# Linear attention with a Mish block on one core: denominators of the first block in front of kv, modulation's columns later, norms moved between engines

## The chip, the cores and the metric

The kernel runs on one core of one Trainium2 chip. The core has TensorE (matrix products), VectorE, ScalarE and GpSimd (work on tiles of 128 partitions), and SyncE, whose queue only starts transfers. The profile calls them PE, DVE, ACT, POOL and SP; PEld is TensorE's loading of the stationary operand. Each engine takes its instructions in the order in which the program issues them, and waits on semaphores for what other engines and transfers deliver. The metric is the device time of one execution in microseconds (us), lower is better.

## The reference

S = 2048 rows, D = 512 columns, F = 1792, 32 heads of 16. Cut to what matters:

```python
mod = (silu(c) @ w_mod).reshape(1, 6, 1, -1)
sa, ca, ga, sb, cb, gb = (mod[:, i] for i in range(6))
h = layernorm(x) * (1 + ca) + sa
q, k, v = heads(h @ wqkv)
pq, pk = phi(q), phi(k)                  # phi(t) = where(t > 0, t + 1, exp(t)) + 1e-6
kv = einsum("bhsd,bhse->bhde", pk, v)
z = einsum("bhsd->bhd", pk)
o = einsum("bhqd,bhde->bhqe", pq, kv) / (einsum("bhqd,bhd->bhq", pq, z)[..., None] + 1e-6)
x = x + ga * (merge(o) @ wo)
h = layernorm(x) * (1 + cb) + sb
x = x + gb * (mish(h @ w1 + b1) @ w2)
```

## The kernel before

The 2048 rows are four blocks b = 0 to 3 of 512, each of four tiles t of 128 rows by 512 columns. Nearly every tile in SBUF comes from one pool of 101 buffers of 2 KB a partition (`sb`), so a load can wait until an older tile is no longer read. PSUM has eight banks in three groups: "acc" (4), "h" (3) and "tp" (1). Products are made in three passes from a high and a low half of each operand: `mm3` multiplies high by high, high by low and low by high. `split` makes the halves: ScalarE copies the high half, and one step later VectorE subtracts it from the operand to get the low half (names ending in h and l).

The order of work is written out by hand. Work beside the products is written as generators; `spawn` puts one in a list, and `tick()`, which stands between the units of TensorE's work, runs each listed generator on to its next `yield`, in the order of spawning. `spawn_idle` does the same for work that comes at the end of each tick. So the position of a `yield`, of a `spawn` or of a call decides where an instruction stands in its engine's queue.

The stages:

1. The block 0 norm, its K, and then for b = 1 to 3 the K products (`k_unit`), phi of K, and the sum of K's outer products with the normalized x (`g_unit`, in four "acc" banks, gacc). `ln_side(b)` (L423) normalizes block b's x beside the products of the block before: statistics on VectorE, the power -1/2 on GpSimd (`ln_rstd`, L199), the apply on ScalarE (`ln_apply`, L208; its other form, L210, is VectorE's). The transposes of block b + 1 (`transpose`, L237) read all four tiles.
2. `q_sevens` makes Q of blocks 0 and 1 together, in seven products instead of eight per pair of halves. A partial product stays in its bank; VectorE reads it (cq, L356), and then another product is added onto the same bank. `beside_q(n)` is called between those products: it starts loads of x, spawns `kv_side` and `mod_side`, and ticks. `mod_side(order, per)` loads columns of `w_mod` and, three ticks after a load, reduces each on VectorE to a column of mc (`mod_col`, L175, out wm). After column 23 it spawns `bcast_row`, which transposes gb on TensorE (bank "tp"), copies it on ScalarE and sends it out and back through two GpSimd transfers, to have gb on all partitions; after column 19 it makes 1 + cb.
3. The masked product kv (kv_ps, L940, then two VectorE passes, L943) and its split. Then Q of block 2 (`q_unit(2, g)`), beside it the denominators of blocks 0 and 1, and m = kv times wo (m_ps). `attend(b, wait, queue)` (L784) is a generator: first 32 small products on TensorE sum q over the heads (den, L789, bank "tp"); then VectorE adds a constant and takes the reciprocal (L793, L794), one transfer writes it to DRAM (rden_d, L796), and four transfers read it back, spread over 16 partitions a head (rd, L800), both on `queue`, GpSimd's if none is named; after `wait` more ticks VectorE multiplies q by rd (L808) and the result is split (qs).
4. Q of block 3, in its middle the output units of block 0 (`o_unit`, out o: 12 matmuls of qs by m); `norm_first` and `norm_each` norm the result for the Mish block, with sums by ScalarE (`act_sums`, L220, L221) and GpSimd's power. `rows(g, wait)` (L686) loads two column groups of w1 on SyncE's queue, waits that many steps, makes their sums on VectorE (L697 to L700) and splits them; `early_rows` holds the first two.
5. The output units of blocks 1 to 3, and then the Mish block. `pair_unit(0, g, ...)` makes two column groups of blocks 0 and 1 in seven products, again adding products onto banks that VectorE has read (cb, L1044); `two_pairs` interleaves the first two pairs. Beside each pair run `w2_job` (w2 times gb, stored to DRAM), `rows` of a later pair, the second products (`d_unit`, oacc), and `norm_tile` for one of the eight tiles of blocks 2 and 3: tiles with even t on ScalarE (sums, then the apply), with odd t on VectorE (statistics, then the apply). `norm_next()` spawns the next one: at the start of each pair from the third on (g = 2 and up), and in `trail`, whose unit runs late in a pair. After the last pair the normed tiles are read back.
6. The same products for blocks 2 and 3, and the second product of those in sevenths.

Of the kernel before, what the change touches and what calls it, by code (L numbers as in the profile page):

```python
# [25 lines left out]
def block_kernel(ctx: ExitStack, tc: tile.TileContext, x, wqkv, wo, w1, b1t, w2, c, wmodt, out):  # L26
    nc = tc.nc
    act, dve, pool, pe, sp = nc.scalar, nc.vector, nc.gpsimd, nc.tensor, nc.sync
# [13 lines left out]
    def ps(tag, name, shape=(P, 512)):  # L42
        return psp.tile(list(shape), F32, tag=tag, name=name, bufs=PBUFS[tag])
# [6 lines left out]
    def spawn(gen):  # L50
        fresh.append(iter(gen))

    def spawn_idle(gen):

        idle_work.append(gen)
# [45 lines left out]
    def load_wmod(i):  # L101
        wm[i] = sb(f"wm_{i}")
        sp.dma_start(wm[i], wmodt[P * i:P * (i + 1), :])
# [102 lines left out]
    def ln_apply(key, b, j, t, dst, engine):  # L206
        if engine is act:
            act.activation(dst, t, AF.Identity, bias=nb[key, b][:, j:j + 1], scale=rs[key, b][:, j:j + 1])  # L208
        else:
            engine.tensor_scalar(dst, t, mv[key, b][:, j, 0:1], rs[key, b][:, j:j + 1],  # L210
                                 op0=ALU.subtract, op1=ALU.mult)
# [195 lines left out]
    def mod_side(order, per):  # L407

        steps = [order[n:n + per] for n in range(0, len(order), per)]
        for n in range(len(steps) + 3):  # L410
            for i in steps[n] if n < len(steps) else ():
                load_wmod(i)
            if n >= 3:
                for i in steps[n - 3]:
                    mod_col(i, sc_row)
                    for lo, name in (8, "ga"), (20, "gb"):
                        if i == lo + 3:
                            spawn(bcast_row(lo, name))
                    if i == 19:
                        plus_one(16, 20)  # L420
            yield

    def ln_side(b):  # L423
        for j in range(4):
            ln_stats("x", b, j, xt["x", b, j])
            if j == 3:
                ln_eps("x", b)
                ln_rstd("x", b)
            yield
        ln_shift("x", b)  # L430
        for j in range(4):
            t = xt["x", b, j]
            ln_apply("x", b, j, t, t, act)
            if j % 2:
                yield

# [249 lines left out]
    def rows(g, wait):  # L686

        r = [sb(f"w1p_{g}_{i}", F32, (P, 4, P)) for i in range(2)]
        for i in range(2):
            f = 2 * g + i  # L690
            sp.dma_start(r[i], w1[:, P * f:P * (f + 1)].rearrange("(k p) f -> p k f", p=P))
        for _ in range(wait):
            yield
        a11, a12, a21, a22 = [r[i][:, 2 * k:2 * k + 2, :] for i in range(2) for k in range(2)]
        s12, s34 = [sb(f"s{n}_{g}", F32, (P, 4, P)) for n in (12, 34)]
        s1, s2, s3, s4 = s12[:, 0:2, :], s12[:, 2:4, :], s34[:, 0:2, :], s34[:, 2:4, :]
        dve.tensor_tensor(s1, a21, a22, op=ALU.add)  # L697
        dve.tensor_tensor(s2, s1, a11, op=ALU.subtract)
        dve.tensor_tensor(s3, a11, a21, op=ALU.subtract)
        dve.tensor_tensor(s4, a12, s2, op=ALU.subtract)  # L700
        yield
        keep, todo = {}, []
        op_rows[g] = keep
        for name, v, parts in (("a1", r[0], ("a11", "a12")), ("s12", s12, ("s1", "s2")), ("s34", s34, ("s3", "s4")),
                               ("a22", a22, ("a22",))):
            half = split(f"{name}_{g}", v, keep, name)
            next(half)
            todo.append((name, half, parts))
            if len(todo) == 2:
                yield  # L710
                for name, half, parts in todo:
                    run(half)
                    for i, part in enumerate(parts):
                        op_a[g, part] = [h[:, 2 * i:2 * i + 2, :] for h in keep[name]]
                todo = []
# [16 lines left out]
            for i, part in enumerate(parts):  # L732
                op_a[g, part] = [h[:, 2 * i:2 * i + 2, :] for h in halves]

    early_rows = [rows(g, 1) for g in range(2)]

    for b in range(1, NB):
        last = b == NB - 1
# [45 lines left out]
    def attend(b, wait, queue=pool):  # L784

        p = ps("tp", f"den_{b}")[:, 0:P]
        for g in range(4):
            for t in range(4):
                pe.matmul(p[32 * t:32 * (t + 1), :], hmask[:, g, :], pq[b, g][:, P * t:P * (t + 1)],  # L789
                          start=g == 0, stop=g == 3)  # L790
        yield
        rden = cst.tile([P, P], F32, tag="rden", name=f"rden_{b}", bufs=2)
        dve.tensor_scalar(rden, p, tiny_den[:, 0:1], 1.0, op0=ALU.add, op1=ALU.mult)  # L793
        dve.reciprocal(rden, rden)  # L794
        d = drp.tile([32, 512], F32, name=f"rden_d_{b}")
        queue.dma_start(bass.AP(tensor=d.tensor, offset=d.offset, ap=[[P, 4], [512, 32], [1, P]]), rden)  # L796
        rd = []
        for g in range(4):
            r = sb(f"rd_{b}_{g}")
            queue.dma_start(r, bass.AP(tensor=d.tensor, offset=d.offset + 8 * g * 512,  # L800
                                     ap=[[512, 8], [0, 16], [1, 512]]))
            rd.append(r)
        for _ in range(wait):
            yield
        parts = []
        for g in range(4):
            t = pq[b, g]
            dve.scalar_tensor_tensor(t, t, TINY, rd[g], op0=ALU.add, op1=ALU.mult)  # L808
            parts.append(split(f"qs_{b}_{g}", t, qs, (b, g)))
            next(parts[-1])  # L810
            if g % 2:
                yield
                run(parts.pop(0))
                run(parts.pop(0))
# [100 lines left out]
    def kv_side():  # L915

        for k in range(4):
            dve.scalar_tensor_tensor(zs[k], gacc[k], mc[:, 4 + k:5 + k], zs[k], op0=ALU.mult, op1=ALU.add)
            if k % 2:
                yield  # L920

    def beside_q(n):
        if n < 4:
            load_x(1, n, "r")
        else:
            load_x(2, n - 4, "r")
        if n == 1:
            spawn(kv_side())
            spawn(mod_side([20, 21, 22, 23, 16, 17, 18, 19], 2))
        tick()  # L930

    q_sevens(beside_q)
    load_x(2, 3, "r")
    kvs = {}
    kv_ps = ps("acc", "kv_ps")
    for g in range(4):
        for k in range(4):
# [6 lines left out]
                          kv_ps.rearrange("p (g m) -> p g m", g=4)[js, :, js],  # L944
                          bmask[js, js].unsqueeze(1).to_broadcast([64, 4, 64]), op=ALU.mult)
    spawn(split("kv", kv, kvs, 0))
    attending = attend(0, 3)
    for g in range(4):
        q_unit(2, g)
        if g == 0:  # L950
            next(attending)
            next(attending)
        if g == 1:
            spawn(attending)
        if g == 2:
            spawn(attend(1, 4))
        if g == 1:
            spawn(mod_side(range(12, 16), 1))
        load_x(3, g, "r")
        if g == 2:  # L960
            for k in range(4):
                m_ps = ps("acc", f"m_ps_{k}")
                mm3(m_ps, [h[:, P * k:P * (k + 1)] for h in kvs[0]], wos[k], True, True)
                spawn(split(f"m_{k}", m_ps, ms, k))
        tick()
    for g in range(4):
        q_unit(3, g)
        tick()
        if g == 1:
            for t in range(4):  # L970
                o_unit(0, t)
                spawn(norm_first(t))
                if t == 1:
                    spawn(attend(2, 5))
                tick()
            spawn_idle(early_rows[1])
    act.preload_act_table_set("mish")

    order = {8: [(0, 0), (0, 2)], 9: [(0, 1)], 10: [(0, 3), (1, 0)], 11: [(1, 2)], 12: [(1, 1)], 13: [(1, 3)]}
    for b in range(1, NB):  # L980
        for t in range(4):
            n = 4 * b + t
# [180 lines left out]
    begun = [pair_begin(0, g, ("tp" if g else "h", "acc")) for g in range(2)]  # L1163
# [8 lines left out]
    def norm_next():  # L1172
        if tiles:
            spawn(tiles.pop(0))

    def trail(f, side=None):
        def unit():
            if side is not None:
                norm_next()
                spawn(side)  # L1180
            d_unit(0, f, f)
            ahead(1, f)
        return unit

    for g in range(1, G):
        for f in (2 * g, 2 * g + 1):
            spawn(w2_job(f))
        if g == 1:
            two_pairs(0, 0, 1, begun, (lambda: None, trail(0, rows(3, 2))))
            store_rows(0)  # L1190
        else:
            norm_next()
            pair_unit(0, g, g % 2, (trail(2 * g - 3), trail(2 * g - 2, rows(g + 2, 2) if g + 2 < G else ())))
        if g < KEPT:
            store_rows(g)
        if g == G - 1:
            for n in range(8):
                load_back("n", nd, 2 + n // 4, n % 4)
# [104 lines left out]
    for n, g in enumerate(pairs):  # L1303
# [18 lines left out]
        if n == 0:  # L1322
            begun = [pair_begin(L, pairs[i], ("tp" if i else "h", "acc")) for i in range(2)]
# [79 lines left out]
```

## Time and profile before

| | before |
|---|---|
| median of 3 runs (lowest to highest) | 502.89 us (502.24 to 505.9) |
| the profiled execution | 501.73 us, span 499.9 us |
| granted TensorE clock in it | 1.00 |
| DMA packets, bytes, mean rate | 66765, 98.58 MB, 197 GB/s |

The profiled execution's own time is its span and the 1.8 us around it. Lines of the timeline read: start, duration, engine, line, operation, out<-in, shape, count, and in brackets the idle time of that engine before the instruction and what ended it. Times count from the span's start. A matmul's end is modelled, so start times are what can be compared.

The page's row of TensorE's busy time in 40 equal slices, and of the DMA engines':

```profile
PE   7999999999998999999999999999999999999997
...
DMA  8714544157556407279799887989997614688512
```

Each digit is the busy share of 12.5 us in tenths. TensorE is at 9 nearly throughout; the transfers are light from 25 to 180 us, where the attention is computed, and heavy from 230 to 375 us, in the Mish block.

### The profile page before, as it was taken

The page shows a single profiled execution, that of the slowest core. Times are in us where ns is not written, and L with a number is a line of the kernel's source. Part 1 is how long each engine was busy: PE and PEld are TensorE (multiplying, and loading weights), DVE is VectorE, ACT ScalarE, POOL GpSimd, SP SyncE. Part 2 cuts the span into 40 slices and gives each one's busy share as a digit, 9 for nine tenths or more (in the row PEclk, how much of TensorE's full clock was granted, in tenths as well). Part 3 has the DMA queues.
Part 4 walks back from the last instruction along what each step waited for, and adds up shares of the span by engine and source line. Part 5 has one row for each costly group of instructions (what it writes and reads, how often), then busy time and mean ns, then how long its engine had stood idle before and what let it go on. Part 6 is the DMA issues. An engine that isn't in the chain of part 4 may idle for free.

```text
span 499.9 us, 7705 instructions
## 1 busy us (share of the span) xinstructions
PE 489.5 (98%) x2640; PEld 411.1 (82%) x2640; DVE 367.9 (74%) x713; ACT 298.7 (60%) x535; POOL 145.2 (29%) x246
## 2 busy tenths in 40 slices
PE   7999999999998999999999999999999999999997
PEld 6787888877786878887888888888788888899997
DVE  6886888999759599977777663679832666759871
ACT  6878587866453879747776655278154555568200
POOL 4573120000022414103224415124554400445200
PEclk9999999999999999999999999999999999999999
DMA  8714544157556407279799887989997614688512
GB/s 310 280 43 113 140 118 93 49 146 249 171 132 156 118 18 251 88 259 358 259 346 333 292 258 195 356 239 372 388 339 190 190 45 126 164 216 224 135 43 85
DMA packets 66765, 98.58 MB, mean 197 GB/s; under 512 B 7405, under 2 KB 31861, under 8 KB 66726
## 3 DMA queue, kind: packets, MB, share of 16 engines
q0 software_dynamic: 29360, 45.31, 33.3%
q1 hardware_dynamic: 37220, 52.51, 31.7%
q8 instruction: 21, 0.34, 0.3%
q10 hardware_dynamic: 146, 0.26, 0.1%
q14 instruction: 18, 0.15, 0.1%
HBM read 62.92 MB, written 33.03 MB: 192 GB/s over the span
## 4 chain that ended last, share of the span: by engine, by line
PE 80%; DVE 10%; ACT 4%; DMA 3%; issue 1%; POOL 1%; POOLq 0%; DVEq 0%; ACTq 0%
PE p_a L1039 18%; PE p_s L1039 7%; PE oacc L76 5%; PE oacc L75 5%; PE oacc L74 5%; PE m L76 5%; PE m L75 5%; PE m L74 5%; PE gacc L75 3%; PE gacc L76 3%; PE gacc L74 3%; PE pk L76 2%; PE pk L74 2%; PE pk L75 2%; PE pq_a L345 2%; DMA rden_d<-rden 1%
## 5 line engine op out<-in xcount | busy, mean ns | idle before, releaser
L1044 DVE TENSOR_TENSOR cb<-p_s,u 128x512 f32<-128x512 f32 x28 | 19.2, 686 | 12.1 <-ACT u L1080 12.1
L1074 ACT ACTIVATE u<-p_a 128x512 f32<-128x512 f32 x12 | 7.2, 599 | 34.5 <-PE p_a L1039 34.5
L199 POOL TENSOR_TENSOR rs_n<-rs_n,half 128x1 f32<-128x1 f32 x16 | 10.1, 631 | 48.9 <-DVE rs_n L225 36.3
L1031 ACT ACTIVATE ub<-cb,b1c 128x512 f32<-128x512 f32 x28 | 20.0, 717 | 5.7 <-DVE cb L1044 5.6
L1049 ACT ACTIVATE u<-p_a 128x512 f32<-128x512 f32 x14 | 8.4, 597 | 23.9 <-PE p_a L1039 23.9
L1301 POOL DMA_DIRECT2D wt_m<-w2t x20 | 14.0, 704 | 27.0 <-DVE cb L1044 14.7
L896 ACT ACTIVATE hf_n<-tp_n,mc 128x512 f32<-128x512 f32 x16 | 11.7, 769 | 12.8 <-PE tp_n L894 12.8
L684 POOL DMA_DIRECT2D w2b<-w2d x20 | 10.6, 548 | 22.9 <-PE tp_n L894 5.0
L1080 ACT ACTIVATE u<-p_a 128x512 f32<-128x512 f32 x14 | 8.4, 598 | 14.1 <-PE p_a L1039 14.1
L1044 DVE TENSOR_TENSOR c<-p_a,u 128x512 f32<-128x512 f32 x14 | 9.6, 689 | 9.0 <-PE p_a L1039 4.4
L259 DVE SCALAR_TENSOR_TENSOR ku<-e_k,relu_k 128x512 f32<-128x512 f32 x16 | 11.0, 687 | 7.0 <-ACT relu_k L257 6.9
L256 ACT ACTIVATE e_k<-pk 128x512 f32<-128x512 f32 x16 | 9.6, 597 | 9.5 <-PE pk L76 9.5
L796 POOL DMA_DIRECT2D rden_d<-rden x3 | 2.2, 735 | 43.5 <-DVE rden L794 43.5
L678 POOL DMA_DIRECT2D wb<-w2d x14 | 9.9, 711 | 15.4 <-PE p_a L1039 12.4
L808 DVE SCALAR_TENSOR_TENSOR q<-q,rd 128x512 f32<-128x512 f32 x16 | 10.4, 682 | 5.2 <-DMA rd<-rden_d 5.2
L199 POOL TENSOR_TENSOR rs_x<-rs_x,half 128x1 f32<-128x1 f32 (+1 forms) x10 | 7.4, 744 | 23.3 <-DVE rs_x L194 22.5
L208 ACT ACTIVATE x<-x,nb_x,rs_x 128x512 f32<-128x512 f32 x15 | 11.5, 809 | 4.3 <-DVE nb_x L203 3.8
L1008 ACT ACTIVATE u<-p_a,b1c 128x512 f32<-128x512 f32 x14 | 9.6, 682 | 6.7 <-PE p_a L1039 6.7
L268 POOL DMA_DIRECT2D ku<-ku x8 | 7.2, 894 | 19.8 <-DVE ku L259 19.8
L731 POOL DMA_DIRECT2D a1b<-rd_a x10 | 5.4, 541 | 19.8 <-PE p_a L1039 8.1
L190 DVE BATCH_NORM_STATS2 st_x<-x 128x6 f32<-128x512 f32 x13 | 8.9, 682 | 3.0 <-DMA x<-in_x_dram 3.0
L820 DVE TENSOR_TENSOR r<-o,r 128x512 f32<-128x512 f32 x16 | 10.8, 675 | 0.0
(1569 smaller groups left out, 1978.8 us busy)
## 6 DMA issues: line engine op xcount, KB each, us to landing
wm<-in_wmodt_dram SPq DMA_DIRECT2D x24, 256.0 KB, 4.4
w2b<-w2d POOLq DMA_DIRECT2D x20, 256.0 KB, 5.7
wt_m<-w2t POOLq DMA_DIRECT2D x20, 256.0 KB, 3.9
r<-in_x_dram SPq DMA_DIRECT2D x16, 256.0 KB, 2.7
x<-in_x_dram SPq DMA_DIRECT2D x15, 256.0 KB, 4.8
w1p<-in_w_dram SPq DMA_DIRECT2D x14, 256.0 KB, 4.2
w2r<-in_w_dram SPq DMA_DIRECT2D x14, 256.0 KB, 4.3
wb<-w2d POOLq DMA_DIRECT2D x14, 256.0 KB, 5.3
```

Of the source, the lines that this page charges most:

```text
L74: pe.matmul(o, st[0], mv[0], start=start, stop=False)
L75: pe.matmul(o, st[0], mv[1], start=False, stop=False)
L76: pe.matmul(o, st[1], mv[0], start=False, stop=stop)
L199: pool.tensor_tensor(y, y, half[:, lo:hi], op=ALU.pow)
L208: act.activation(dst, t, AF.Identity, bias=nb[key, b][:, j:j + 1], scale=rs[key, b][:, j:j + 1])
L259: dve.scalar_tensor_tensor(dst, e, 1.0, r, op0=ALU.min, op1=ALU.add)
L820: dve.tensor_tensor(r, p, r, op=ALU.add)
L896: act.activation(hf[b, j], p, AF.Identity, bias=mc[:, 12 + j:13 + j], scale=mc[:, 16 + j:17 + j])
L1031: act.activation(u, p, AF.Mish, bias=b1c[:, f:f + 1])
L1039: pe.matmul(p, st, mv, start=onto is None and c == 0 and i == 0, stop=c == 1 and i == 2, skip_group_check=onto is not None)
L1044: dve.tensor_tensor(out, p, u, op=ALU.add)
L1301: pool.dma_start(v, w2t[g][:, :, SUM[name], :])
```

## The change

Six edits, each a move:

- `ln_side(2)`: the apply of tiles 2 and 3 goes to VectorE. `ln_side(3)` stays on ScalarE.
- `mod_side` for columns 20 to 23 and 16 to 19 is spawned at the fifth call of `beside_q` instead of the second, so loads, columns, 1 + cb and the broadcast of gb all come three ticks later.
- `attend(0, 3)`: its 32 denominator products stand in front of the kv products on TensorE; its reciprocal and transfers stand right behind kv's two passes, in front of Q of block 2.
- `attend(2, 5)` starts its five transfers from SyncE's queue instead of GpSimd's.
- `rows(1)` is spawned before block 0's output units instead of behind them, and waits three steps more: its loads stand four ticks earlier, its sums one.
- `two_pairs` spawns no norm tile, so the eight tiles start with the third pair, and tiles with even t come at the start of a pair, those with odd t in its trail.

```diff
@@ ln_side
-            ln_apply("x", b, j, t, t, act)
+            ln_apply("x", b, j, t, t, act if b > 2 or j < 2 else dve)
@@ block_kernel
-    early_rows = [rows(g, 1) for g in range(2)]
+    early_rows = [rows(g, 3 * g + 1) for g in range(2)]
@@ beside_q
         if n == 1:
             spawn(kv_side())
+        if n == 4:
             spawn(mod_side([20, 21, 22, 23, 16, 17, 18, 19], 2))
@@ block_kernel
     kvs = {}
+    attending = attend(0, 3)
+    next(attending)
     kv_ps = ps("acc", "kv_ps")
...
     spawn(split("kv", kv, kvs, 0))
-    attending = attend(0, 3)
+    next(attending)
     for g in range(4):
         q_unit(2, g)
-        if g == 0:
-            next(attending)
-            next(attending)
         if g == 1:
             spawn(attending)
...
         if g == 1:
+            spawn_idle(early_rows[1])
             for t in range(4):
                 o_unit(0, t)
                 spawn(norm_first(t))
                 if t == 1:
-                    spawn(attend(2, 5))
+                    spawn(attend(2, 5, sp))
                 tick()
-            spawn_idle(early_rows[1])
...
-    def trail(f, side=None):
+    def trail(f, side=None, norm=True):
         def unit():
             if side is not None:
-                norm_next()
+                if norm:
+                    norm_next()
                 spawn(side)
...
-            two_pairs(0, 0, 1, begun, (lambda: None, trail(0, rows(3, 2))))
+            two_pairs(0, 0, 1, begun, (lambda: None, trail(0, rows(3, 2), False)))
```

No instruction is added or dropped, apart from the form of two norms; the output is the same computation.

## The prediction

> **What bounds the kernel now.** I read the page first, then the table of waits on TensorE, then the timeline of TensorE around each wait, then VectorE, ScalarE and GpSimd at the same places.
>
> ```profile
> PE 489.5 (98%) x2640; PEld 411.1 (82%) x2640; DVE 367.9 (74%) x713; ACT 298.7 (60%) x535; POOL 145.2 (29%) x246
> ```
>
> TensorE is busy 98% of the span, so an edit that gives it no less work can only win back its waits. The table of waits on TensorE is short; these are the entries that the change can touch:
>
> ```profile
> PE o L76 <- DVE qs_2l L88: 1.0, 1, 1.0
> PE p_s L1039 <- DVE nb_n L229: 0.8, 1, 0.8
> PE o L74 <- ACT qs_2h L82: 0.7, 1, 0.7
> ...
> PE pq_s L345 <- DVE cq L356: 0.7, 1, 0.7
> ...
> PE tp_x L237 <- ACT x L208: 0.4, 1, 0.4
> ...
> PE tp_n L894 <- ACT n L208: 0.2, 1, 0.2
> ```
>
> These idle times are too small, because a matmul's end is modelled. What counts is from start to start: a matmul of 512 columns follows the one before it 0.23 us later when nothing is waited for, and whatever exceeds that is lost. I price each wait so. The change does no matmul less and none more. It is therefore a sum of waits, each to be checked for what comes late next.
>
> **1. The norm of the third block's x (tiles 2 and 3 to VectorE).** TensorE, eight transposes and the matmul after them, in the place that waits and in the next that does not:
>
> ```profile
> 47.30 0.39 PE L237 MATMUL tp_x<-ident,x 128*128 128x128 f32 x2
> ...
> 49.05 0.47 PE L74 MATMUL gacc<-pk_0h,xn_0h 128*128 128x512 f32 x1
> ...
> 54.60 1.03 PE L237 MATMUL tp_x<-ident,x 128*128 128x128 f32 x8
> ...
> 55.39 0.48 PE L74 MATMUL gacc<-pk_2h,xn_2h 128*128 128x512 f32 x1
> ```
>
> 49.05 - 47.30 = 1.75 against 55.39 - 54.60 = 0.79: 0.96 us lost, put down to ScalarE's norm. What VectorE has there, and what such a norm costs on it:
>
> ```profile
> 45.61 0.69 DVE L90 SCALAR_TENSOR_TENSOR pk_1l<-ku,pk_1h 128x512 fp32r<-128x512 f32 x1 [1.15 <-ACT pk_1h L82]
> ...
> 239.25 0.55 DVE L210 TENSOR_SCALAR r<-r,mv_n,rs_n 128x512 f32<-128x512 f32 x1
> ```
>
> In program order the two norms fall just ahead of pk_1l, where VectorE idles 1.15 us waiting for ScalarE. Two at 0.55 are 1.10: the hole hides them, and both tiles are ready at about 45.6, before TensorE asks at 47.5. Without the hole pk_1l would be 1.1 later, at 47.4; the gacc matmuls that read it come behind those of the first tile, after 50. Gain 0.96.
>
> **2. Modulation's columns three ticks later.** TensorE, and VectorE before it:
>
> ```profile
> 124.36 0.39 PE L345 MATMUL pq_s<-qt_0h,qs_1l 128*128 128x512 f32 x1
> 125.43 0.50 PE L345 MATMUL pq_s<-hT_x_2h,qs_0h 128*128 128x512 f32 x1 [0.69 <-DVE cq L356]
> 125.77 0.40 PE L345 MATMUL pq_s<-hT_x_2l,qs_0h 128*128 128x512 f32 x1
> ```
>
> ```profile
> 122.86 0.69 DVE L175 SCALAR_TENSOR_TENSOR wm<-wm,sc_row 128x512 f32<-128x512 f32 x1
> ...
> 124.69 1.28 DVE L356 TENSOR_TENSOR cq<-pq_s,qu 128x512 f32<-128x512 f32 x2
> ```
>
> Lost: 1.07 - 0.23 = 0.84, and the matmul after a wait takes 0.34 instead of 0.23, so 0.96 in all. The product onto the same bank may start only when cq has read it. Two columns stand between VectorE's backlog and cq; a pass takes about 0.61 there, two 1.23. Without them cq comes 1.23 earlier, which exceeds the wait. Gain 0.96. All eight columns now fall into the four Q units of block 2; VectorE idles there (below), and what they feed, the broadcast of gb and 1+cb, is used behind block 1's output units, near 185. The broadcast row's transpose (gb_ps) moves from beside block 2's Q to beside block 3's, with its two transfers on GpSimd, now behind block 1's. It takes the bank "tp" after the second denominator. VectorE reads that bank two passes after the second rd product, which stands at 147.32 and moves 4.0 forward (part 3): by 145. The transpose comes one Q unit (12 matmuls, 2.7 us) before the first output unit, at 152.18 - 1.92 - 2.7 = 147.5. No wait is counted; the cover is 2.5 us.
>
> **3. First denominators in front of kv.** By here TensorE is 1.92 early.
>
> ```profile
> 128.37 2.09 PE L940 MATMUL kv_ps<-zs,wv 128*64 128x64 f32 x64
> ...
> 133.33 1.08 PE L789 MATMUL den<-q,hmask 128*32 128x128 f32 x32
> ```
>
> ```profile
> 134.48 0.35 DVE L793 TENSOR_SCALAR rden<-den,tiny_den 128x128 f32<-128x128 f32 x1 [2.90 <-PE den L789]
> ```
>
> ```profile
> 136.11 0.74 POOL L796 DMA_DIRECT2D rden_d<-rden  x1 [42.59 <-DVE rden L794]
> ```
>
> ```profile
> 145.74 0.69 DVE L808 SCALAR_TENSOR_TENSOR q<-q,rd 128x512 f32<-128x512 f32 x1 [4.35 <-DMA rd<-rden_d]
> 147.32 0.69 DVE L808 SCALAR_TENSOR_TENSOR q<-q,rd 128x512 f32<-128x512 f32 x1 [0.89 <-DMA rd<-rden_d]
> ...
> 155.74 0.68 DVE L88 TENSOR_TENSOR qs_2l<-q,qs_2h 128x512 fp32r<-128x512 f32 x1
> ```
>
> ```profile
> 152.18 0.39 PE L74 MATMUL o<-m_0h,qs_0h 128*128 128x512 f32 x1
> ...
> 160.32 1.08 PE L789 MATMUL den<-q,hmask 128*32 128x128 f32 x32
> ```
>
> Two output units of 12 matmuls take 160.32 - 152.18 = 8.14 where 24 at 0.23 are 5.52: 2.6 lost, the largest wait. Its chain runs from the denominators over the reciprocal and two transfers to qs_2l. In the changed order: den starts at 128.37 - 1.92 = 126.45, kv follows at 127.5 and ends at 129.6, kv's two masked passes on VectorE (0.4 each by estimate, half as wide as the 0.69 ones) end near 130.4, the reciprocal stands behind them and the transfer goes out 136.11 - 134.48 = 1.63 later, at 132.1. That is 4.0 earlier, 2.1 of it relative to TensorE. From the issue to the end of qs_2l the order of work is the same (156.42 - 136.11 = 20.3), so qs_2l ends at 152.4. TensorE wants it as ninth matmul, at 152.18 - 1.92 + 8 x 0.23 = 152.1. About 0.3 us remain, and 0.1 for the restart. The bounds: 0 if the transfers land as much sooner as TensorE needs, 1.5 if each lands 1.2 us later among the loads of the columns; I take 0.4, by the transfers' own rows. Gain 2.2. What the swap delays is kv itself, by the 1.0 of den:
>
> ```profile
> 140.52 0.39 PE L76 MATMUL m_ps<-wos_0h,kvl 128*128 128x512 f32 x1
> ```
>
> This matmul is the first that reads kvl; 1.92 earlier it wants it at 138.6. On VectorE stand in front of it rden to 131.7, four columns, four q and the split itself, nine passes at 0.6: 137.1. Slack 1.5.
>
> The rule of the Trainium skill that speaks against this is in SBUF — State Buffer, section "SBUF: two separate sides": descriptors of a transfer issued from GpSimd cannot be written while VectorE holds the shared port in its fast modes. It is weighed as a rival below, from rows of GpSimd.
>
> **4. attend(2) on SyncE, rows(1) earlier.** VectorE, then TensorE:
>
> ```profile
> 173.01 0.16 DVE L229 TENSOR_TENSOR nb_n<-sums_n,rs_n 128x1 f32<-128x1 f32 x1 [4.36 <-POOL rs_n L199]
> ```
>
> ```profile
> 186.94 0.39 PE L75 MATMUL o<-m_2l,qs_2h 128*128 128x512 f32 x1
> 187.45 0.50 PE L76 MATMUL o<-m_2h,qs_2l 128*128 128x512 f32 x1
> ```
>
> VectorE stands 4.36 us because the power for a norm is queued on GpSimd behind block 2's transfers, which wait for each other. Moved to SyncE's queue these no longer block it; rows(1)'s sums (1.5 us) also leave the backlog that follows. SyncE's queue now waits for the reciprocal with rows(1)'s two loads ahead of it and the first two w2 loads behind; the latter are used only behind block 1's output units, so nobody waits. The backlog made TensorE lose 0.51 - 0.23 + 0.11 = 0.39 at qs_2l and 0.2 at tp_n; TensorE comes some 4 us earlier, VectorE as much and 4 more. Gain 0.6.
>
> **5. No norm tile in the first two pairs.** TensorE, then ScalarE:
>
> ```profile
> 235.02 0.39 PE L1039 MATMUL p_a<-b_3h,a_2l 128*128 128x512 f32 x1
> 236.19 0.47 PE L1039 MATMUL p_s<-t_0h,s_2h 128*128 128x512 f32 x1 [0.78 <-DVE nb_n L229]
> ```
>
> ```profile
> 231.92 0.62 ACT L220 ACTIVATE scrap_n<-r 128x512 f32<-128x512 f32 x1
> ...
> 233.39 0.67 ACT L1008 ACTIVATE u<-p_a,b1c 128x512 f32<-128x512 f32 x1
> ```
>
> Lost: 1.17 - 0.23 = 0.94, with the restart 1.05. The releaser named, nb, is a neighbour: the bank is freed by the cb sum just before it on VectorE, which waited for ScalarE's Mish behind the sums of the norm, 233.39 - 231.92 = 1.47. Without them cb is 1.47 earlier, more than 0.94. Gain 1.05. The tiles move half a pair, so in pairs 2 to 5 a ScalarE norm now opens each pair and a VectorE norm trails it; counted at nothing, because ScalarE has this hole in each of the pairs, 34.5 / 12 = 2.9 us, into which the 1.47 fit:
>
> ```profile
> L1074 ACT ACTIVATE u<-p_a 128x512 f32<-128x512 f32 x12 | 7.2, 599 | 34.5 <-PE p_a L1039 34.5
> ```
>
> The trailing place loses the 1.47 on ScalarE for one pass of statistics and the 0.55 of the apply on VectorE. All eight tiles are still stored before the last pair ends; if the cover fails, it costs what rival (c) says.
>
> **The sum**: 0.96 + 0.96 + 2.2 + 0.6 + 1.05 = 5.8 us. The profiled execution took 501.73, so it would take 496.0; the median of the runs is 1.16 above it: 502.89 - 5.8 = **497.1 us**. Of the size of the parts, the third is the least sure: its bounds give 496.7 to 498.2.
>
> **Rivals.** (a) The first output unit still waits as long: 2.2 less, 499.3. For it: transfers slow down in company, and SyncE now loads columns beside them. Against: they start 2.1 closer. Chance 0.13.
>
> (b) GpSimd's transfers are held up while VectorE works:
>
> ```profile
> 141.32 1.77 POOL L800 DMA_DIRECT2D rd<-rden_d  x3 [0.24 <-issue]
> ...
> 153.90 2.40 POOL L800 DMA_DIRECT2D rd<-rden_d  x4 [2.62 <-DMA rden_d<-rden]
> ```
>
> The first were issued while VectorE idled (its 4.35 above), 0.59 each; the second while it worked, 0.60 each. In the new order VectorE works through both. If each of the first two issues took 2.5 us longer, the second rd and with it qs_2l would come 5 us later: 502.1. Chance 0.03, since the rows show no such effect. [...]
>
> (c) The moved norms start a wait in each of the four pairs, for instance VectorE's apply waiting for GpSimd's power in front of cb: 4 x 1.05 = 4.2, so 501.3. For it: that very sum made the wait in part 5. Against: the table has this wait once, though pairs 2 to 5 had norms in both places. Chance 0.09.
>
> (d) On the other side: the columns' loads come late.
>
> ```profile
> 136.40 4.87 SPq L103 DMA_DIRECT2D wm<-in_wmodt_dram  x2
> ```
>
> ```profile
> wm<-in_wmodt_dram SPq DMA_DIRECT2D x24, 256.0 KB, 4.4
> ```
>
> These two loads stood until a buffer came free. Should the loads of columns 20 to 23 now be served only then, 20 and 21 land at 141.3 - 1.9 + 4.4 = 143.8, where VectorE takes them at 131.7, and kv's split, the reciprocals' products and all behind wait: kvl at 149.2, 10.6 later than TensorE wants it. That is 10.6 against 5.8 won and some of part 3 saved: 507; with 22 and 23 another such pair later, 513. It decides once the columns come over 1.5 us late, costs 1 us each from there, and turns the gain at 7. Against: in the table of all waits no engine waits for a column's load, though each was asked for only three ticks ahead, as now. Chance 0.10.
>
> (e) The change doesn't do what it says, for instance other work of equal size fills each hole: 502 or so. Chance 0.03.
>
> **Numbers.** Forecast 0.62. Its own range is 496.0 to 498.6, with the bounds of part 3 and half a microsecond for the rest. Range: 495.8 to 501.5, which takes in (a) and (c). A measurement here tells about 1%, 5.0 us: faster by more needs under 497.9, which is most of the forecast's range: 0.53. Within 1%: the rest of it with (a), (b), (c), (e), 0.37. Slower: (d), 0.10.
>
> **What would show it.** In the table of waits on TensorE all six lines gone, but for a rest under 0.7 at qs_2l of block 0; den standing before kv_ps at about 126.5; the rden transfer at about 132; nb no longer waiting on GpSimd near 170; kvl before 138. Wrong if columns wait for a DMA, if m_ps or gb_ps appears among TensorE's waits, or if p_s waits in later pairs.

## The result, and the profile after

| | before | after |
|---|---|---|
| median (lowest to highest, 6 runs each, on one chip) | 503.19 us (502.07 to 505.9) | 495.07 us (494.47 to 495.5) |
| the profiled execution (its span) | 501.73 us (499.9) | 494.9 us (493.1) |
| granted TensorE clock in it | 1.00 | 1.00 |

The ratio of the times is 0.9833, 95% interval 0.9807 to 0.9859: faster by 1.7%. 497.1 was forecast with a range of 495.8 to 501.5. The direction is right, the time lies 0.7 below the range. The medians differ by 8.1 us, the two profiled executions by 6.8; the forecast was 5.8.

The page of after, busy time, and the table of waits on TensorE, whole (engine, line, tile, releaser: us in total, times, longest):

```profile
PE 486.7 (99%) x2640; PEld 411.6 (83%) x2640; DVE 370.1 (75%) x715; ACT 298.3 (60%) x533; POOL 143.4 (29%) x241
```

```profile
PE warm L136 <- POOL ones L130: 1.1, 1, 1.1
PE tp_x L474 <- ACT x L208: 1.1, 3, 0.4
PE pk L519 <- ACT hT_x_0h L500: 0.4, 1, 0.4
PE pk L522 <- DVE hT_x_0l L512: 0.3, 1, 0.3
PE gacc L75 <- DVE pk_0l L90: 0.2, 1, 0.2
PE sc_bc L142 <- ACT c L140: 0.2, 1, 0.2
```

All six lines that the prediction listed are gone, and nothing new stands in their place. What is left belongs to the first 25 us. How much each place gave is read by setting starts of the same matmul in both timelines against each other. TensorE's timeline of after:

```profile
47.48 1.03 PE L237 MATMUL tp_x<-ident,x 128*128 128x128 f32 x8
48.27 0.48 PE L74 MATMUL gacc<-pk_0h,xn_0h 128*128 128x512 f32 x1
...
124.03 0.39 PE L345 MATMUL pq_s<-hT_x_2l,qs_0h 128*128 128x512 f32 x1
...
126.61 1.08 PE L789 MATMUL den<-q,hmask 128*32 128x128 f32 x32
...
152.03 0.39 PE L76 MATMUL o<-m_2h,qs_2l 128*128 128x512 f32 x1
...
152.94 0.39 PE L74 MATMUL o<-m_0h,qs_0h 128*128 128x512 f32 x1
...
229.59 0.39 PE L1039 MATMUL p_a<-b_3h,a_2l 128*128 128x512 f32 x1
229.82 0.39 PE L1039 MATMUL p_s<-t_0h,s_2h 128*128 128x512 f32 x1
...
489.74 0.28 PE L76 MATMUL m<-wt_m,l_m_4l 128*128 128x256 f32 x1
```

and two rows of before that the prediction did not need:

```profile
157.50 0.39 PE L74 MATMUL o<-m_0h,qs_0h 128*128 128x512 f32 x1
...
496.24 0.28 PE L76 MATMUL m<-wt_m,l_m_4l 128*128 128x256 f32 x1
```

| up to | before | after | earlier by | so this part gave | forecast |
|---|---|---|---|---|---|
| tp_x begins | 47.30 | 47.48 | -0.18 | (start-up) | 0 |
| first gacc | 49.05 | 48.27 | 0.78 | part 1: 0.96 | 0.96 |
| second pq_s after the wait | 125.77 | 124.03 | 1.74 | part 2: 0.96 | 0.96 |
| block 0's second output unit | 157.50 | 152.94 | 4.56 | part 3: 2.82 | 2.2 |
| the last p_a in front of p_s | 235.02 | 229.59 | 5.43 | part 4: 0.87 | 0.6 |
| last matmul | 496.24 | 489.74 | 6.50 | part 5: 1.07 | 1.05 |
| end of the span | 499.9 | 493.1 | 6.8 | (after the last matmul) 0.3 | 0 |

The chain of part 3 on VectorE and GpSimd of after:

```profile
136.70 0.68 DVE L88 TENSOR_TENSOR kvl<-kv,kvh 128x512 fp32r<-128x512 f32 x1
...
142.22 0.69 DVE L808 SCALAR_TENSOR_TENSOR q<-q,rd 128x512 f32<-128x512 f32 x1 [0.38 <-DMA rd<-rden_d]
...
150.63 0.68 DVE L88 TENSOR_TENSOR qs_2l<-q,qs_2h 128x512 fp32r<-128x512 f32 x1
```

```profile
132.28 0.74 POOL L796 DMA_DIRECT2D rden_d<-rden  x1 [39.55 <-DVE rden L794]
...
137.96 1.77 POOL L800 DMA_DIRECT2D rd<-rden_d  x3 [0.22 <-issue]
```

The transfer was forecast for 132.1 and goes out at 132.28; kvl was forecast to end at 137.1 and ends at 137.38. qs_2l was forecast to end at 152.4 and to be wanted at 152.1. It ends at 151.31 and is wanted at 152.03, so the rest of 0.4 that the forecast kept does not exist. The second product with rd starts 142.22 - 132.28 = 9.9 after the first transfer's issue, where it was 147.32 - 136.11 = 11.2 before: the transfers landed sooner.

So the sum of the waits was 1.0 too small by the profiles, and the medians moved 1.3 more than the profiled executions did. The experiments ask mostly where that 1.3 is.

### The profile page after: what moved, and what is told of

It reads as the page before. It is cut to its first block, busy times and chain, and to the rows that moved or that the text cites. A ratio compares the mean times of both kernels' runs of the same rounds, so it can differ in the third digit from the quotient of the medians.

```text
span 493.1 us, 7710 instructions
## 1 busy us (share of the span) xinstructions
PE 486.7 (99%) x2640; PEld 411.6 (83%) x2640; DVE 370.1 (75%) x715; ACT 298.3 (60%) x533; POOL 143.4 (29%) x241
## 4 chain that ended last, share of the span: by engine, by line
PE 96%; DVE 1%; ACT 1%; DMA 1%; issue 0%; ACTq 0%
PE p_a L1039 19%; PE p_s L1039 8%; PE oacc L76 5%; PE oacc L74 5%; PE oacc L75 5%; PE m L76 5%; PE m L75 5%; PE m L74 5%; PE o L74 3%; PE gacc L75 3%; PE o L76 3%; PE gacc L76 3%; PE o L75 3%; PE gacc L74 3%; PE pq_a L345 3%; PE pk L76 2%
## 5 line engine op out<-in xcount | busy, mean ns | idle before, releaser
L199 POOL TENSOR_TENSOR rs_n<-rs_n,half 128x1 f32<-128x1 f32 x16 | 11.4, 710 | 60.2 <-DVE rs_n L194 35.5
L259 DVE SCALAR_TENSOR_TENSOR q<-e_q,relu_q 128x512 f32<-128x512 f32 x16 | 10.7, 686 | 2.6 <-ACT relu_q L257 2.6
L208 ACT ACTIVATE x<-x,nb_x,rs_x 128x512 f32<-128x512 f32 x13 | 10.0, 809 | 4.3 <-DVE nb_x L203 3.8
L808 DVE SCALAR_TENSOR_TENSOR q<-q,rd 128x512 f32<-128x512 f32 x16 | 10.5, 685 | 1.7 <-DMA rd<-rden_d 1.7
```

What stands on the lines that cost most here:

```text
L199: pool.tensor_tensor(y, y, half[:, lo:hi], op=ALU.pow)
L259: dve.scalar_tensor_tensor(dst, e, 1.0, r, op0=ALU.min, op1=ALU.add)
```

## The experiments

Theory T: the slower executions of the kernel before spend their excess in the wait of block 0's first output unit, which the change removes, so the median gains more than a fast profile shows. Its rival R: they spread generally, and the excess is not tied to an edit.

### The kernel before once more

> The kernel before, unchanged, profiled a second time. The runs shown of it lie between 502.07 and 505.9 us, the execution profiled so far at 501.73. Theory T: what a slower execution has in excess sits in the wait of block 0's first output unit for the reciprocals' transfers, so this profile, if it is slower than 501.73 by d, shows 2.6 + d us lost between 152 and 160 us and nothing new elsewhere. Rival R: the excess is spread or sits at the start or the end, outside the waits that the change removes; then the loss at the output unit is 2.6 again.

Measured: 503.46 (501.87 to 505.94, 12 runs), ratio 1.0008 (0.9992 to 1.0024). The profiled execution took 502.78, 1.05 more than the first. TensorE's timeline:

```profile
152.47 0.39 PE L75 MATMUL o<-m_0l,qs_0h 128*128 128x512 f32 x1
153.97 0.50 PE L76 MATMUL o<-m_0h,qs_0l 128*128 128x512 f32 x1 [1.12 <-DVE qs_0l L88]
```

From start to start 1.50, where the first profile had 152.85 - 152.41 = 0.44. These 1.06 us are the whole difference, as T has it. The runs' mean granted clocks (the share of TensorE's full clock, averaged over an execution) brought something that neither theory had. Over 61 runs of the kernel before on two chips:

| mean granted clock of the run | runs | median us |
|---|---|---|
| 1.000 | 20 | 502.47 |
| 0.999 | 8 | 502.76 |
| 0.997 | 25 | 503.94 |
| 0.993 | 8 | 504.63 |

In 11 more runs on a third chip, beside the last two experiments, 5 had 0.993 or 0.997. Of after's six runs four had 1.000 and two 0.999. So a profile with a lower clock was wanted. Two more profiles of the kernel before:

> The kernel before, unchanged, for another profile: if its clock is 0.997 or less, the stretch of the span in which the granted clock is down is to be read from it. Theory G: the stretch begins within 5 us behind the wait at block 0's first output unit (152 to 157), lasts about 3.4 us at half clock and costs about 1.7 us. Rival H: the stretch lies elsewhere, for instance behind the kv matmuls (128 to 131), at the start, or at the end of the span.

> The same once more. If its clock is 1.0 it shows the same chain of waits as the first profile of the kernel before, with the wait for qs_0l, qs_2h and qs_2l of block 0 at 2.5 to 3.7 us in all. Theory T: what of the time differs from the other profiles of the kernel before is lost within the first output unit, between 152 and 158 us, or in the clock.

The first took 503.27 with a clock of 0.997, the second 501.94 with 1.000. Stretches of four us of the first (length, TensorE's busy time and matmuls, granted clock, DMA share, GB/s), and its timeline behind the wait:

```profile
152.00:156.00 4.00, 2.56 (x10) 1.00 0.23 58
156.00:160.00 4.00, 3.04 (x10) 0.76 0.99 240
160.00:164.00 4.00, 4.00 (x42) 0.81 1.11 244
```

```profile
158.07 0.58 PE L74 MATMUL o<-m_0h,qs_0h 128*128 128x512 f32 x1
158.44 0.63 PE L75 MATMUL o<-m_0l,qs_0h 128*128 128x512 f32 x1
158.87 0.63 PE L76 MATMUL o<-m_0h,qs_0l 128*128 128x512 f32 x1
...
161.43 0.44 PE L76 MATMUL o<-m_2h,qs_2l 128*128 128x512 f32 x1
```

One microsecond behind the last of the three waits the clock falls to half: matmuls of 512 columns follow each other at 158.87 - 158.44 = 0.43 instead of 0.23, for eight of them. 161.43 - 158.07 = 3.36 us for the work of 8 x 0.227 = 1.8: 1.5 us lost, in one place, near 158, as theory G had it and rival H not. That is a second price at the same place, and it is paid in some executions only. Against the first profile this execution loses 2.2 us here, 0.66 of it in a longer wait for qs_0l; about 0.6 comes back, since block 2's units find their operands ready, and 503.27 - 501.73 = 1.5 stay. The second of these two, with the full clock, has the waits of the first profile within 0.25 us and takes 0.2 us longer.

The same stretches of the repeat above, whose wait is the longest of the four profiles:

```profile
152.00:156.00 4.00, 2.15 (x9) 1.00 0.28 79
156.00:160.00 4.00, 3.04 (x13) 1.00 0.92 230
```

TensorE was less busy there, and the clock stayed full. So the length of the wait alone does not say whether the clock falls.

### Which edit removes it

> The changed kernel with the first denominators back behind the first Q unit of block 2. Both theories: the wait at qs_2l of block 0 comes back, some 2.2 to 2.6 us, so about 497.5 us, against 495.1. Theory T: the runs spread again over more than 1.5 us and the median lies another 1 us higher, at 498.5. Rival R: the spread stays at 1 us and the median at 497.5.

> The changed kernel with modulation's columns spawned at the second call again. Expected from the sum: the wait of 0.96 us in front of the product onto pq_s comes back, 496.0 us. Theory T: its runs stay within about 1 us of each other. It also puts four columns in front of kv's passes again, which has 2.35 us of idle VectorE to hide them, so no second wait.

> The changed kernel with parts 2 and 3 both put back (columns early, denominators behind kv); x's norms, SyncE for attend(2) and no norm tile in the first two pairs stay. Theory C (the wait at block 0's first output unit exists only when both the columns and the order of kv stand in front of the reciprocals, and the fall of the granted clock comes with that wait): the wait is back (2.5 us or more, qs_2l and qs_2h of block 0 in the table), pq_s 0.95 too, and the granted clock is 0.997 or less in about 4 runs of 10. Median 495.1 + 0.95 + 2.6 + 1.0 = 499.7, spread 2 us or more, although each of the two put back alone gave only 496.7 and 495.9 with a clock of 1.0. Rival A (the parts add up): 495.1 + 1.6 + 0.8 = 497.5, clock 1.0 or 0.999 in all.

Denominators behind kv again, everything else as in after:

```diff
+    next(attending)
     for g in range(4):
         q_unit(2, g)
+        if g == 0:
+            next(attending)
+            next(attending)
```

with the two earlier lines removed. Columns early again: `if n == 4:` removed, so that `mod_side` is spawned at n == 1. The third kernel has both.

| put back in after | median (lowest to highest, runs) | ratio to before | clocks |
|---|---|---|---|
| nothing | 495.07 (494.47 to 495.5, 6) | 0.9833 (0.9807 to 0.9859) | 0.999, 1.0 |
| denominators | 496.66 (496.24 to 497.15, 4) | 0.9874 (0.986 to 0.9888) | 1.0 |
| columns | 495.87 (495.65 to 496.23, 4) | 0.9859 (0.9845 to 0.9872) | 1.0 |
| both | 500.8 (499.04 to 502.18, 9) | 0.994 (0.992 to 0.996) | 0.993 to 0.996 in seven, 0.999, 1.0 |

With the denominators back alone the output unit still does not wait. The wait stands at another place, where m_ps wants kvl:

```profile
139.31 0.50 PE L76 MATMUL m_ps<-wos_0h,kvl 128*128 128x512 f32 x1 [0.74 <-DVE kvl L88]
```

With the columns back alone only the pq_s wait (0.7 in the table) is back. With both, the longest waits on TensorE behind the start are:

```profile
PE o L76 <- DVE qs_2l L88: 1.0, 1, 1.0
PE o L74 <- ACT qs_2h L82: 0.7, 1, 0.7
PE pq_s L345 <- DVE cq L356: 0.7, 1, 0.7
```

and behind them the profile, of clock 0.996, again has eight matmuls at half clock:

```profile
157.35 0.63 PE L74 MATMUL o<-m_0h,qs_0h 128*128 128x512 f32 x1
157.77 0.63 PE L75 MATMUL o<-m_0l,qs_0h 128*128 128x512 f32 x1
...
160.33 0.59 PE L75 MATMUL o<-m_2l,qs_2h 128*128 128x512 f32 x1
```

So the parts don't add up: 1.6 and 0.8 alone, 5.7 together. T had expected the wait and the spread back with the denominators alone; neither came. Each of the two edits is enough to take the wait at the output unit away, and with it, by the mean clocks, go the half-clock stretches. Theory C's 499.7 for both missed 1.1: it counted the lower clock in 4 runs of 10, it came in 7 of 9.

The variants ran in batches beside the kernel before, on other chips than after, and its median there was 502.87 to 504.08. A difference between medians of two batches therefore holds to about 1 us: the 1.6 and the 0.8 are rough, the 5.7 is clear of it.

### The wait filled with work

> The kernel before with nine more matmuls of 512 columns in block 0's first output unit, each with a stationary tile of zeros, so that they add nothing to the output: four in front of the matmul that waits for qs_2h and five in front of the one that waits for qs_2l, 9 x 0.23 = 2.1 us of work put into about 2.5 us of waiting. One more pass of ScalarE writes the zeros near 112 us. Theory G (TensorE's idling there is what lowers the granted clock): the wait ends when it ended, TensorE hardly idles, the granted clock is 1.0 or 0.999 in all runs, and the median falls by about 1 although work was added: 502 against 503 of the kernel before, runs within 2 us. Rival H (the clock falls for another reason): clock 0.997 or less in about 4 runs of 10 as before, median 503 to 504. Rival I (the added matmuls cost their time): 504 or more.

```diff
@@ o_unit of the kernel before, b = 0, t = 0, g = 2
+                for _ in range(4):
+                    pe.matmul(p, zst, ms[0][0], start=False, stop=False)
                 pe.matmul(p, st[0], ms[g][0], start=False, stop=False)
                 pe.matmul(p, st[0], ms[g][1], start=False, stop=False)
+                for _ in range(5):
+                    pe.matmul(p, zst, ms[0][0], start=False, stop=False)
                 pe.matmul(p, st[1], ms[g][0], start=False, stop=False)
```

Measured: 502.48 (501.58 to 504.7, 12 runs) beside 503.68 of the kernel before, ratio 0.9988 (0.9971 to 1.0005). Its timeline and the stretch:

```profile
154.30 1.09 PE L834 MATMUL o<-m_0h,zst 128*128 128x512 f32 x4
...
155.72 1.32 PE L838 MATMUL o<-m_0h,zst 128*128 128x512 f32 x5
156.88 0.46 PE L839 MATMUL o<-m_2h,qs_2l 128*128 128x512 f32 x1
```

```profile
152.00:156.00 4.00, 3.54 (x16) 1.00 0.28 70
```

The wait ends where it ended (156.88 against 156.48, and 0.38 of that was lost in front already, at qs_0l), TensorE is busy 3.54 of 4 us instead of the 2.56 of the profile at clock 0.997 above, and all 12 runs have a clock of 0.999 or 1.0, where 11 of the 19 runs of the kernel before beside them had 0.997 or 0.993. That is theory G's main point, and rivals H and I fall: nine added matmuls cost no time that the runs show. The median is 1.2 lower, but the interval of the ratio just reaches 1, and the runs spread over 3.1 us, not within 2: the clock is one cause of the spread; the landing of the transfers, which this edit leaves, is probably the other.

### One edit alone in the kernel before

> The kernel before with the denominators in front of kv and nothing else of the change. The question is whether the 1.3 us of median that the change won beyond the sum of the profiled waits hang on the first output unit's wait for the reciprocals' transfers. Theory T (they do): with the denominators alone moved, TensorE does not wait at qs_2l of block 0 (2.6 us lost in the profile of before, 3.6 in its repeat), the other five waits stay (pq_s 0.7, tp_x 0.4, p_s 0.8, o <- qs_2h 0.7, tp_n 0.2 by the table), and the median falls by more than the wait: 503.0 - 2.6 - 1.3 = 499.1, the runs within 1.5 us of each other and the granted clock 1.0 or 0.999 in all of them. Rival R (the excess is a general spread of the kernel before, which this edit leaves): the median falls by the 2.6 alone, to 500.4, the runs still spread over 3 us or more, and some runs still show a clock of 0.997 or less. Rival S (the edit alone is worth less, since the columns' loads still run beside the transfers): a wait of 0.5 to 1.5 stays at qs_2l and the median is 500.5 to 502.

> The kernel before with the eight columns of modulation spawned three ticks later and nothing else. Theory T: the columns that no longer stand in front of the reciprocals shorten the same chain, so that the wait at qs_2l of block 0 goes too (2.6), the pq_s wait goes (0.95), and at most 0.9 comes back as a wait of m_ps for kvl, as when only the denominators were put back: 2.7 to 3.5 us by the profile, another 1.3 by the median with the clock drops: 498.2 to 499, runs within 1.5 us, clock 1.0 in all. Rival R (edits add up as the forecast had it, this one is worth its own 0.96): median 502.0, the wait at qs_2l of block 0 grows to about 2, spread 3 us as before, clock 0.997 or less in some of the runs.

The denominators alone: 501.06 (499.89 to 501.73, 6 runs), ratio 0.9948 (0.993 to 0.9965). The columns alone: 499.46 (499.29 to 500.15, 5 runs), ratio 0.9921 (0.9904 to 0.9938). All clocks 0.999 or 1.0, and no wait at block 0's output unit in either: T's point holds for both. The kernel before took 504.08 beside them, not the 503.0 that T counted from. Against 504.08 the columns alone won 4.6, within T's 4.0 to 4.8, and the denominators alone 3.0, where T had 3.9, R 2.6. The runs of the denominators spread over 1.8 us, not R's 3 or more, and S's wait at qs_2l of block 0 did not stay. There another wait takes part of the gain; it is shown here on TensorE, and its cause on VectorE:

```profile
186.54 0.50 PE L76 MATMUL o<-m_2h,qs_2l 128*128 128x512 f32 x1 [1.64 <-DVE qs_2l L88]
```

```profile
172.09 0.16 DVE L229 TENSOR_TENSOR nb_n<-sums_n,rs_n 128x1 f32<-128x1 f32 x1 [4.37 <-POOL rs_n L199]
```

TensorE comes 2.4 earlier to this wait (184.51 for 186.94 at the matmul in front), VectorE's nb only 173.01 - 172.09 = 0.92, since it still hangs on GpSimd's queue. For the columns alone R (502.0) is far off: this edit is the larger of the two by itself, with 0.7 of wait at m_ps as T's expectation had it.

### The two norms

> The changed kernel with all four norms of the third block's x on ScalarE again. The forecast's term: 0.96 lost at tp_x near 47 us, and nothing gained back later, since TensorE waits nowhere behind it: profile 494.9 + 0.96 = 495.9, median 495.1 + 0.96 = 496.0, table of waits with tp_x <- ACT x L208 0.4 back. Rival (a later wait had been hidden or a later slack takes it up): median within 0.3 of 495.1, or over 496.6.

> The changed kernel with the norm tile in the first two pairs again. The forecast's term: p_s waits 0.94 with 0.11 of restart near 230 us, 1.05 in all: profile 494.9 + 1.05 = 495.9, median 496.1, table of waits with p_s L1039 <- DVE nb_n (or ACT) 0.8 back once. Rival: the wait was an effect of what came before it in the kernel before (VectorE's backlog of that place, 4 us less now), and does not come back: median within 0.3 of 495.1.

All four norms on ScalarE: 496.1 (495.59 to 497.39, 5 runs), 1.0 more than after. The norm tile back in the first two pairs: 495.88 (495.74 to 496.56, 4 runs), 0.8 more. Each wait is back at its place, the first from the one kernel, the second from the other:

```profile
48.47 0.77 PE L237 MATMUL tp_x<-ident,x 128*128 128x128 f32 x5 [0.37 <-ACT x L208]
```

```profile
231.46 0.47 PE L1039 MATMUL p_s<-t_0h,s_2h 128*128 128x512 f32 x1 [0.78 <-DVE nb_n L229]
```

Both are near the forecast's prices (0.96 and 1.05). The p_s wait is the same 0.94 from start to start (231.46 - 230.29 - 0.23, by the p_a in front), although VectorE's backlog near 173 is gone: it has its own cause.

### SyncE and rows(1)

> The changed kernel with attend(2)'s transfers on GpSimd's queue again. Expected from the sum: VectorE stands for some 4 us behind the power, and TensorE loses up to 0.6 us near qs_2l of block 2 and tp_n: 495.7 us; 0 if the earlier start of everything covers it. Theory T: this chain is not what varies, so the spread stays near 1 us; rival: transfers issued by GpSimd vary wherever they stand, and the spread grows here as well.

> The changed kernel with rows(1) started where it was before, behind block 0's output units; attend(2) stays on SyncE. Theory P (the two halves of part 4 stand in for each other, each alone frees VectorE soon enough): no wait over 0.3 us at block 2's output unit, median 495.1 to 495.3. Rival Q (rows(1) is the half that carries part 4's 0.6, since putting attend(2) back on GpSimd cost 0.15 only): a wait of 0.4 or more behind 180 us, median 495.5 to 495.8.

> The changed kernel with both halves of part 4 put back: attend(2) on GpSimd and rows(1) late. Theory P (they stand in for each other; with neither, VectorE stands about 4.4 us for a norm's power near 167 us while TensorE comes 4 us earlier than in the kernel before, as where the denominators alone were moved and 1.8 us were lost at block 2's output unit): 1.5 to 2.5 us lost between 178 and 196 us, median 496.6 to 497.5. Rival (they add up, the forecast's 0.6 at most): median 495.2 to 495.7.

```diff
@@ first: attend(2) on GpSimd
-                    spawn(attend(2, 5, sp))
+                    spawn(attend(2, 5))
@@ second: rows(1) late
-    early_rows = [rows(g, 3 * g + 1) for g in range(2)]
+    early_rows = [rows(g, 1) for g in range(2)]
...
-            spawn_idle(early_rows[1])
             for t in range(4):
...
                 tick()
+            spawn_idle(early_rows[1])
```

The first alone gave 495.22 (494.98 to 495.69, 5 runs): T's narrow spread holds, and the 0.6 does not show in the median, though its profiled execution loses 0.75 near 196. Both gave 495.64 (495.22 to 496.62, 5 runs). VectorE stands for the norm's power again with both:

```profile
167.27 0.16 DVE L229 TENSOR_TENSOR nb_n<-sums_n,rs_n 128x1 f32<-128x1 f32 x1 [4.28 <-POOL rs_n L199]
```

TensorE loses only 0.28 behind it: at tp_n it is 0.23 ahead of after (186.46 for 186.69), at the output matmul behind it 0.05 late (187.53 for 187.48). Theory P had 1.5 to 2.5 there and falls; the rival's 495.2 to 495.7 holds. Of the two waits that part 4 was priced by, the one at tp_n comes back and the one at qs_2l of block 2 doesn't.

The second alone gave 500.24 (499.35 to 501.32, 6 runs), ratio 0.9942 (0.9925 to 0.996): 5.2 more, missed by both theories. Its SyncE queue, VectorE and TensorE:

```profile
161.31 0.69 SPq L796 DMA_DIRECT2D rden_d<-rden  x1
163.91 2.60 SPq L800 DMA_DIRECT2D rd<-rden_d  x4
166.60 0.97 SPq L691 DMA_DIRECT2D w1p<-in_w_dram  x2
```

```profile
174.50 0.42 DVE L697 TENSOR_TENSOR s<-w1p 128x256 f32<-128x256 f32 x1 [6.77 <-DMA w1p<-in_w_dram]
```

```profile
176.78 0.43 PE L789 MATMUL den<-q,hmask 128*32 128x128 f32 x8 [1.95 <-DVE q L259]
```

With attend(2) on SyncE and rows(1) late, rows(1)'s loads are queued behind transfers that wait for the reciprocal. They leave at 166.60, in after they leave at 141.07, ahead of them:

```profile
141.07 2.01 SPq L691 DMA_DIRECT2D w1p<-in_w_dram  x2
```

VectorE stands 6.77 us for them, with phi of Q and the splits queued behind; TensorE then waits 1.95 at den and 1.7 at qs_2l. Four of the six runs have a clock of 0.993 to 0.997, although block 0's output unit does not wait here; the profiled run has 1.0, so where the clock falls in the others is not shown. So early rows(1) is not shown to be a gain of its own. It is what keeps the move to SyncE from costing 5.2 us. Both halves together are worth 0.6 by the medians, but the runs overlap with after's.

## Why the prediction was right, and where it was wrong

**Right.** TensorE's waits bound the kernel, with all edits none of the priced waits is left, and no cover failed. Part 1 and part 2 gave 0.96 each, to the hundredth; part 5 gave 1.07 for 1.05, and undoing part 1, part 2 or part 5 brought back the wait that it was priced by. The bank of gb_ps and kvl, the two covers with least slack, held: neither is in the table of waits. Part 4's condition, that rows(1)'s loads stand ahead of the waiting transfers, is what undoing it confirmed, and the fear that some queue is held up is real there: had it been broken, the change would have won 2.7 instead of 8.1.

**The rivals.** (a) fell: the output unit waits for nothing. (b) fell: GpSimd's three rd issues at 137.96 took 1.77, 0.59 each, as before, and now with VectorE at work throughout. The Trainium skill, SBUF — State Buffer, section "SBUF: two separate sides", gives about 620 ns for such a transfer alone and about 3100 beside a `tensor_copy` of VectorE. VectorE's passes at this place each take in two tensors and are no copies, so no run here tests that figure. (c) fell: no wait at p_s in any pair. (d) fell: no engine waits for a column's load. (e) fell with the gain.

**Wrong: the baseline and part 3.** The forecast of 497.1 was 2.0 too high: 1.1 in the profiled execution (496.0 for 494.9) and 1.0 in the distance from it to the median. Two steps failed. The first is "the median of the runs is 1.16 above it: 502.89 - 5.8 = 497.1". It took the distance between the median and a fast profile for a constant and carried it over to after. It was 1.2 to 1.5 before and is 495.07 - 494.9 = 0.2 after. The distance was itself a product of the wait that part 3 removes: the varying landing of the transfers (0.44 to 1.50 from start to start at qs_0l) and, in 33 of 61 runs, a lower mean clock (a run of 0.997 was profiled, and one of 0.996 with both edits back; each shows one stretch at half clock, about 1.5 us lost; a run of 0.993 was not profiled). The experiments that remove the wait by either edit, or only fill it, have 0.999 or 1.0 in every run, and the one that restores the wait has the lower clock in seven of nine.

The second is a size: part 3's "Two output units of 12 matmuls take 8.14 where 24 at 0.23 are 5.52: 2.6 lost" was right for the one execution, but "About 0.3 us remain, and 0.1 for the restart" was not, because the transfers landed 1.3 sooner; the profiled gain was 2.82, and by the medians of undoing parts 2 and 3 together 5.7, for 0.96 + 2.2 forecast. Why the transfers land sooner was not tried by itself. The profiles show when they do: from the first transfer's issue to the second product with rd it is 11.2 to 12.3 us in the six executions without either edit, of part 2 or of part 3 (four of the kernel before, the filled one, and both put back), and at most 10.5 in the ten with one edit or both.

Part 4 measured 0.87 by the profile for 0.6; put back it cost 0.6 by the medians and 0.28 on TensorE in its profile, so its size stays open.

Put back by groups, the medians give 1.0 (part 1), 5.7 (parts 2 and 3), 0.6 (part 4) and 0.8 (part 5): 8.1 in all, the measured gain. By each batch's ratio to the kernel before they are 1.3, 5.4, 1.2 and 0.8, 8.7 in all. Each of these has an uncertainty near 1 us by the intervals of the ratios, so the agreement at 8.1 is luck. None of the variants tried is faster than the changed kernel.

## What to carry to other kernels

A wait that depends on a transfer's landing can vary from execution to execution: price it from several profiles, not from the fastest. Here the medians gained 8.1 where the profiled executions gained 6.8. Two edits that shorten the same chain can be alternatives, not terms of a sum: here 1.6 and 0.8 each, 5.7 together. When transfers that wait for something move to another queue, list the loads that are now behind them: here two such loads would have taken back 5.2 of 8.1 us.

## What the runs showed of the hardware that was not expected

The granted clock fell to half for about 3.4 us although TensorE never idled for long: the three waits in front of it were 0.7 to 1.0 us each by the table, and in the four us that hold two of them TensorE was busy 2.56. By the mean clock it fell in 33 of 61 runs of the kernel before, and in none of 12 of the kernel that fills the wait, where the busy time was 3.54. The Trainium skill, TensorE: Matmul & The Clock Gate, section "Part 1: The HAM clock gate (the "warmup" mystery)", has a free-running window of about 3.4 us and half rate after an idle one. The length of the stretch agrees (161.43 - 158.07 = 3.36), and that it comes in some executions and not in others fits. If an idle window is one without any work, the trace does not agree: TensorE was 64% busy here and still lost the clock. The busy share alone does not decide it either: the repeat was busy 2.15 of the same four us, 54%, and kept the clock. Single waits of 0.7 to 1.6 us (m_ps, pq_s, p_s, block 2's output unit) left the clock at 0.999 or more in all 23 runs of five other variants. Where between these the limit lies, and what else it hangs on, was not measured.
